# A one-core SwiGLU kernel: the first x block and the first gate weights loaded in halves of D

## The chip, the cores and the metric

The kernel runs on one NeuronCore of a Trainium2 chip. The metric is the device time of one execution in microseconds (us), lower is better. Where several executions were timed, the median is given.

## The reference

```
x [1, 2048, 512], w_gate [512, 1376], w_up [512, 1376], w_down [1376, 512], all bf16
g = silu(x @ w_gate)
u = x @ w_up
return (g * u) @ w_down
```

D is 512 (the contraction of the first two products), F is 1376 (the contraction of the last one), and S is 2048 tokens.

## The kernel before

**Tiling.** The tokens are cut into 4 chunks `c` of 512. F is cut into 10 whole tiles `ft` of 128 and a rest of 96. A "G" group computes gate for one tile and one chunk: four matmuls, one for each slice `dk` of 128 of D, with 128x128 weights from `w_sb` and 512 tokens of the transposed x (`xT_sb`) as the moving operand. A "U" group does the same for up. ScalarE (ACT) applies silu to the G bank, VectorE (DVE) multiplies it with the U bank and writes `hT_sb`. The rests of F go through groups "X" and "Y". After all chunks, "O" groups compute the down product from `hT_sb` and `wd_sb`, DVE copies them to `o_sb`, and SP stores them.

**Who orders what.** The program is written out by hand for each engine, with semaphores between the engines: `s_P` counts PE's groups, `s_A` ACT's, `s_D` DVE's operations, and every load has a semaphore of its own. PE runs its instructions in the written order. The helper `need(name)` makes PE wait for a load, and `after(eng, n)` for the n-th operation of ACT or DVE.

**The start**, which is where the change lies:

- SP's queue issues, in this order: `xn` (the first 256 tokens of x as they lie in memory, 128 partitions of 2 KB, L108), the gate and the up weights of tile 1 (L92), `x0b` (tokens 256 to 511 through a transposing load, L87), then gate and up weights of tiles 2 and 3, 4 to 6, 7 to the rest, then the other chunks of x and w_down. ACT's queue issues the gate and the up weights of tile 0 (L92). Each of the first four weight loads is a slab of one tile: 512 pieces of 256 bytes, 128 KB.
- PE first runs matmuls on constants whose result nobody reads (L337): `N_WARM` = 6 of 512 columns and `N_FILL` = 2 of 128 columns. Then it waits for `xn` and transposes it, 8 transposes of 128x128 (L346) in 4 groups "T". A group is one block `i` of 128 tokens and one half `h` of D, in the order (i0,h0), (i0,h1), (i1,h0), (i1,h1).
- The 4 groups are copied from PSUM to `xT_sb`: h0 by DVE (L293), h1 by ACT (L280).
- Then PE runs the first halves (tokens 0 to 255) of the groups g0, u0 (in blocks of 128 columns, all four `dk` of a block in turn), g1, u1 (256 columns), and after `x0b` the second halves of all four (L328, 256 columns). From tile 2 on every matmul has 512 columns.

Of the kernel before, what the change touches and what calls it, by code (L numbers as in the profile page):

```python
# [6 lines left out]
BF16 = mybir.dt.bfloat16  # L7
FP32 = mybir.dt.float32

N_WARM = 6  # L10
N_FILL = 2


def bass_standalone__swiglu_ffn__prompt_kernel(nc, x, w_gate, w_up, w_down, out):
    _, S, D = x.shape
    F = w_gate.shape[1]
    P = 128
    KD = D // P
    NFF = F // P
    NFT = NFF + 1  # L20
    F_LAST = F - NFF * P
    SC = 512
# [4 lines left out]
    NR = 3  # L27
    LASTA = 384
    HT = SC // 2
    NXN = HT // P  # L30
    NB = 8
    NSG = 4
# [3 lines left out]
    xf = x[0]  # L36
# [3 lines left out]
    UPH = F + 32  # L40
# [4 lines left out]
    with ExitStack() as es:  # L45
# [4 lines left out]
        xT_sb = sb("xT_sb", [P, KD, S], BF16)  # L50
        w_sb = sb("w_sb", [P, KD, WTOT], BF16)
# [12 lines left out]

        xn_sb = sb("xn_sb", [P, NXN, D], BF16)
        ident = sb("ident", [P, P], BF16)
# [10 lines left out]
        def load_sem(name):  # L77
            loads[name] = sem(f"s_{name}")
            return loads[name]
# [6 lines left out]
        def load_x(eng, name, t0, t1):  # L86
            eng.dma_start_transpose(  # L87
                xT_sb[:, :, t0:t1], xf[t0:t1, :]
            ).then_inc(load_sem(name), 16)

        def load_w(eng, name, src, base, f0, f1):
            eng.dma_start(  # L92
                w_sb[:, :, base + f0:base + f1],
                src[:, f0:f1].rearrange("(k p) f -> p k f", p=P),
            ).then_inc(load_sem(name), 16)

        slabs = [(0, 1), (1, 2), (2, 4), (4, 7), (7, NFT)]
        slab_of = {ft: a for a, b in slabs for ft in range(a, b)}

        def load_slab(eng, a, b):  # L100
            load_w(eng, f"wg{a}", w_gate, 0, a * P, min(b * P, F))
            load_w(eng, f"wu{a}", w_up, UPH, a * P, min(b * P, F - 32))

        def loads_on_scalar(act):
            load_slab(act, *slabs[0])

        def loads_on_sync(sp):
            sp.dma_start(  # L108
                xn_sb[:, :, :].rearrange("p j d -> p (j d)"), xf[0:HT, :].rearrange("(p j) d -> p (j d)", j=NXN)
            ).then_inc(load_sem("xn"), 16)  # L110
            load_slab(sp, *slabs[1])
            load_x(sp, "x0b", HT, SC)
            for a, b in slabs[2:]:
                load_slab(sp, a, b)
            load_w(sp, "wut", w_up, F - (F - 32), F - 32, F)
            for c in range(1, NSC):
                load_x(sp, f"x{c}", c * SC, (c + 1) * SC)
            sp.dma_start(
                wd_sb[:, 0:NFF, :], w_down[0:NFF * P, :].rearrange("(k p) d -> p k d", p=P)
            ).then_inc(load_sem("wd"), 16)  # L120
            for c in range(NSC):
                sp.dma_start(
                    wdt_sb[R * c:R * (c + 1), :, :], w_down[NFF * P:F, :].rearrange("(q p) d -> p q d", p=R)
                ).then_inc(load_sem(f"wdt{c}"), 16)
            sp.dma_start(wdl_sb[:, :], w_down[NFF * P:F, LASTA:D]).then_inc(load_sem("wdl"), 16)
# [7 lines left out]
        def add_group(kind, **what):  # L133
            g = dict(kind=kind, at=len(groups), bank=banks[len(groups) % NB], readers=[], **what)
            groups.append(g)
            return g

        def add_op(eng, g, **what):
            n_read[eng] += 1
            op = dict(g=g, at=n_read[eng], **what)  # L140
            (act_ops if eng == "A" else dve_ops).append(op)
            g["readers"].append((eng, op["at"]))
            return op

        def tview(bank):
            return bank[:, 0:P].bitcast(BF16).rearrange("p (k t) -> p k t", k=2)
# [58 lines left out]
                t_ready[c] = d["at"]  # L205

        xt_ready = {}
        for i in range(NXN):
            for h, eng in enumerate("DA"):
                g = add_group("T", i=i, h=h)  # L210
                op = add_op(
                    eng, g, kind="copy", out=xT_sb[:, 2 * h:2 * h + 2, i * P:(i + 1) * P],
                    src=tview(g["bank"]), stored=(None, 0),
                )
                xt_ready[i, h] = (eng, op["at"])
# [12 lines left out]
        for at in range(NST):  # L228
            j, c = divmod(at, NSC)
            t = c * TPC + j  # L230
            ob = at % NOS
            need = 16 * n_store[ob]
            halves = [(0, D)] if at < NST - 1 else [(0, LASTA), (LASTA, D)]
            for c0, c1 in halves:
                g = add_group("O", t=t, c0=c0, c1=c1, c=c)
                if c0 == 0:
                    quads[j].append(g)
                else:
                    last = g
                eng = "A" if len(halves) == 2 and c0 == 0 else "D"  # L240
                op = add_op(
                    eng, g, kind="copy", out=o_sb[ob][:, c0:c1], src=g["bank"][:, 0:c1 - c0],
# [6 lines left out]
        def rows_of(t):  # L249
            if t < NXN:  # L250
                return of[0:HT, :].rearrange("(p j) d -> j p d", j=NXN)[t]
            return of[t * P:(t + 1) * P, :]

        def on_sync(sp):
            loads_on_sync(sp)
            for t, c0, c1, ob, eng, n in stores:
                sp.wait_ge(s_A if eng == "A" else s_D, n)
                sp.dma_start(rows_of(t)[:, c0:c1], o_sb[ob][:, c0:c1]).then_inc(s_out[ob], 16)
            for i in range(NOS):
                sp.wait_ge(s_out[i], 16 * n_store[i])  # L260
# [6 lines left out]
        def on_scalar(act):  # L267
            loads_on_scalar(act)
            act.activation(adummy[:, 0:4], zero_c, ACT.Silu)  # L269
            for op in act_ops:  # L270
                act.wait_ge(s_P, op["g"]["at"] + 1)
                if op["kind"] == "silu":
                    if op["free"]:
                        act.wait_ge(s_D, op["free"])
                    fn = ACT.Silu
                else:
                    if op["stored"][1]:
                        act.wait_ge(*op["stored"])
                    fn = ACT.Copy
                act.activation(op["out"], op["src"], fn).then_inc(s_A, 1)  # L280
# [15 lines left out]
        def on_tensor(pe):  # L296
            landed = set()

            def need(name):
                if name not in landed:  # L300
                    pe.wait_ge(loads[name], 16)
                    landed.add(name)
# [3 lines left out]
            def after(eng, n):  # L306
                if n > read[eng]:
                    pe.wait_ge(s_A if eng == "A" else s_D, n)
                    read[eng] = n
# [3 lines left out]
                    for eng, n in groups[g["at"] - NB]["readers"]:  # L313
                        after(eng, n)

            def gu_matmuls(g, n0, n1):
                c, ft = g["c"], g["ft"]
                if c > 0:
                    need(f"x{c}")
                if c == 0 and n1 > HT:  # L320
                    need("x0b")
                need(("wg" if g["kind"] == "G" else "wu") + str(slab_of[ft]))
                col = (0 if g["kind"] == "G" else UPH) + ft * P
                for dk in range(KD):
                    if c == 0 and dk % 2 == 0:
                        for i in range(n0 // P, min(n1 // P, NXN)):
                            after(*xt_ready[i, dk // 2])
                    ins = pe.matmul(  # L328
                        g["bank"][:, n0:n1], lhsT=w_sb[:, dk, col:col + P],
                        rhs=xT_sb[:, dk, c * SC + n0:c * SC + n1], start=(dk == 0), stop=(dk == KD - 1),  # L330
                    )
                if n1 == SC:
                    ins.then_inc(s_P, 1)

            def warm(n, width):
                for i in range(n):
                    pe.matmul(banks[NB - 1][:, 0:width], lhsT=ones_w, rhs=ones_m[:, 0:width], start=True, stop=True)  # L337

            warm(N_WARM, SC)
            warm(N_FILL, P)  # L340
            pe.wait_ge(s_J, 1)
            need("xn")
            for g in groups[:NT]:
                for k in range(2):
                    dk = 2 * g["h"] + k
                    ins = pe.transpose(tview(g["bank"])[:, k, :], xn_sb[:, g["i"], dk * P:(dk + 1) * P], ident[:, :])  # L346
                ins.then_inc(s_P, 1)

            g0, u0, g1, u1 = groups[NT:NT + 4]
            for g in (g0, u0):  # L350
                gu_matmuls(g, 0, P)
                gu_matmuls(g, P, HT)
            gu_matmuls(g1, 0, HT)
            gu_matmuls(u1, 0, HT)
            for g in (g0, u0, g1, u1):
                gu_matmuls(g, HT, SC)

            for g in groups[NT + 4:]:
                kind = g["kind"]
# [5 lines left out]
                elif kind == "X":  # L365
                    c = g["c"]
                    need(f"wg{slab_of[NFF]}")
                    need("wut")
                    for dk in range(KD):
                        ins = pe.matmul(  # L370
                            g["bank"][:, :], lhsT=w_sb[:, dk, XC0:XC0 + P],
                            rhs=xT_sb[:, dk, c * SC:(c + 1) * SC],
                            start=(dk == 0), stop=(dk == KD - 1),
                        )
                    ins.then_inc(s_P, 1)
                elif kind == "Y":
                    need(f"wu{slab_of[NFF]}")
                    for dk in range(KD):
                        for c in (2 * g["pi"], 2 * g["pi"] + 1):
# [3 lines left out]
                                rhs=xT_sb[:, dk, c * SC:(c + 1) * SC],  # L383
                                start=(dk == 0), stop=(dk == KD - 1),
# [33 lines left out]
            for j in range(0, TPC, 2):  # L418
# [14 lines left out]
                skip_group_check=True,  # L433
# [35 lines left out]
```

## Time and profile before

| | |
|---|---|
| three timed runs | 120.83, 120.94, 120.31 us; median 120.83 us |
| the profiled execution | 120.32 us |
| span of its trace, first to last instruction | 118.9 us (1.42 us of its time lie around the span) |
| PE busy (matmul) | 115.4 us, 97% of the span |
| DVE, ACT busy | 47.3 us (40%), 31.0 us (26%) |
| loads and stores | 8.84 MB, mean 74 GB/s; the DMA engines are busy through the first 27 us of the span and nearly idle from there to 89 us |

Engines in the profile: PE is the matmul row of TensorE, PEld its weight loads, SPq and ACTq the instructions that SP and ACT issue to DMA queues. L328 is line 328 of the kernel. A row of a timeline gives the start, the duration, what ran, how many were merged, and in brackets the idle time before and what ended it. The duration of one matmul is from its start to the end of its result, so back-to-back matmuls overlap; their pace is the distance from start to start.

### The profile page before, as it was taken

What the parts mean: (1) busy time and instruction counts of PE and PEld (TensorE: products, weight loads), DVE (VectorE), ACT (ScalarE), POOL (GpSimd) and SP (SyncE); (2) the same over time, 40 slices, a digit from 0 to 9 for tenths busy, and PEclk for the clock granted to TensorE, in tenths of its full rate; (3) what the DMA queues carried; (4) which work ended last, traced back from release to release, by engine and by line L of the source; (5) the groups of instructions that cost most, each with busy time, mean ns of one, the idle gap of its engine ahead of it and who ended that gap; (6) DMA issues with size and microseconds to landing.
All of it is one profiled execution on the core that took longest, in us unless ns stands there. A gap on an engine that the chain in (4) does not pass through costs nothing.

```text
span 118.9 us, 1519 instructions
## 1 busy us (share of the span) xinstructions
PE 115.4 (97%) x600; PEld 54.1 (45%) x611; DVE 47.3 (40%) x73; ACT 31.0 (26%) x53; POOL 0.4 (0%) x5
## 2 busy tenths in 40 slices
PE   7999999999999999999999999999999999999993
PEld 2774444444444444444444444344434444444452
DVE  0133443353443444433444334469617422006530
ACT  4344324454234363244262343230000000000001
POOL 1000000000000000000000000000000000000000
PEclk9999999999999999999999999999999999999999
DMA  3999999970000000000000000000004221002412
GB/s 103 271 307 357 264 162 242 328 183 24 0 0 0 6 0 0 0 3 3 0 0 0 6 0 0 0 0 0 0 0 138 88 88 44 0 0 75 145 50 88
DMA packets 17559, 8.84 MB, mean 74 GB/s; under 512 B 10640, under 2 KB 17424, under 8 KB 17552
## 3 DMA queue, kind: packets, MB, share of 16 engines
q1 hardware_dynamic: 16496, 8.48, 26.7%
q10 hardware_dynamic: 1056, 0.26, 1.0%
q8 instruction: 5, 0.08, 0.3%
q14 instruction: 2, 0.02, 0.1%
HBM read 4.81 MB, written 2.10 MB: 58 GB/s over the span
## 4 chain that ended last, share of the span: by engine, by line
PE 97%; issue 1%; DVE 0%
PE bank L328 58%; PE bank L394 29%; PE bank L370 3%; PE bank L337 2%; PE bank L408 2%; PE bank L381 2%; PE bank L346 1%; DVE o_sb L293 0%; PE bank L431 0%
## 5 line engine op out<-in xcount | busy, mean ns | idle before, releaser
L328 PE MATMUL bank<-xT_sb,w_sb 128*128 128x512 bf16 (+2 forms) x338 | 69.7, 364 | 0.4
L328 PEld LDWEIGHTS bank<-xT_sb,w_sb 128*128 128x128 bf16 x344 | 32.8, 98 | 36.4 <-issue 0.2
L289 DVE TENSOR_TENSOR hT_sb<-sg_sb,bank 128x512 bf16<-128x512 f32 x40 | 27.5, 688 | 40.5 <-PE bank L328 36.6
L394 PE MATMUL bank<-wd_sb,hT_sb 128*128 128x512 bf16 (+2 forms) x166 | 34.5, 366 | 0.4 <-issue 0.3
L280 ACT ACTIVATE sg_sb<-bank 128x512 f32<-128x512 f32 x40 | 23.8, 596 | 40.8 <-PE bank L328 40.8
L394 PEld LDWEIGHTS bank<-wd_sb,hT_sb 128*128 128x128 bf16 x170 | 16.1, 98 | 19.1 <-issue 1.3
L293 DVE CAST o_sb<-bank 128x512 bf16<-128x512 f32 (+1 forms) x16 | 10.1, 663 | 22.0 <-PE bank L408 12.3
L280 ACT ACTIVATE o_sb<-bank 128x384 bf16<-128x384 f32 x1 | 0.5, 492 | 37.8 <-PE bank L394 37.8
L289 DVE TENSOR_TENSOR ht_sb<-sgy_sb,bank 32x512 bf16<-32x512 f32 x8 | 5.5, 684 | 0.2
L289 DVE TENSOR_TENSOR ht_sb<-sgx_sb,bank 32x512 bf16<-32x512 f32 x4 | 2.8, 691 | 3.5 <-ACT sgx_sb L280 3.5
L370 PE MATMUL bank<-xT_sb,w_sb 128*128 128x512 bf16 x15 | 4.1, 379 | 0.1
L337 PE MATMUL bank<-const-bfloat16-1.0 128*128 128x512 bf16 (+1 forms) x8 | 2.9, 545 | 0.8 <-PEq L454 0.8
L280 ACT ACTIVATE sgx_sb<-bank 32x512 f32<-32x512 f32 x4 | 2.4, 588 | 4.5 <-PE bank L370 4.5
L408 PE MATMUL bank<-wdt_sb,ht_sb 32*128 32x512 bf16 (+1 forms) x48 | 2.9, 372 | 0.0
L370 PEld LDWEIGHTS bank<-xT_sb,w_sb 128*128 128x128 bf16 x16 | 1.6, 98 | 1.9
L280 ACT ACTIVATE sgy_sb<-bank 64x512 f32<-64x512 f32 x4 | 2.4, 590 | 0.1
L337 PEld LDWEIGHTS bank<-const-bfloat16-1.0 128*128 128x128 bf16 x8 | 1.0, 136 | 2.4 <-issue 2.4
L381 PE MATMUL bank<-xT_sb,w_sb 128*64 128x512 bf16 x16 | 1.9, 382 | 0.0
L408 PEld LDWEIGHTS bank<-wdt_sb,ht_sb 32*128 32x128 bf16 x48 | 1.1, 93 | 1.7 <-issue 0.8
L269 ACT ACT_TABLE_LOAD x1 | 1.3, 1283 | 1.8 <-issue 1.8
L293 DVE COPY xT_sb<-bank 128x256 bf16<-128x256 bf16 x2 | 0.6, 292 | 2.7 <-PE bank L346 2.7
L381 PEld LDWEIGHTS bank<-xT_sb,w_sb 128*64 128x64 bf16 x16 | 0.8, 109 | 1.0 <-DVE hT_sb L289 0.4
(14 smaller groups left out, 4.0 us busy)
## 6 DMA issues: line engine op xcount, KB each, us to landing
out_dram<-o_sb SPq DMA_DIRECT2D x15, 128.0 KB, 1.7
wd_sb<-in_w_down_dram SPq DMA_DIRECT2D x1, 1280.0 KB, 9.2
w_sb<-in_w_gate_dram SPq DMA_DIRECT2D x1, 480.0 KB, 5.9
w_sb<-in_w_up_dram SPq DMA_DIRECT2D x1, 448.0 KB, 6.5
w_sb<-in_w_gate_dram SPq DMA_DIRECT2D x1, 384.0 KB, 4.5
w_sb<-in_w_up_dram SPq DMA_DIRECT2D x1, 384.0 KB, 5.1
wdt_sb<-in_w_down_dram SPq DMA_DIRECT2D x4, 96.0 KB, 7.5
xn_sb<-in_x_dram SPq DMA_DIRECT2D x1, 256.0 KB, 2.8
```

Source lines behind the costliest of these rows:

```text
L269: act.activation(adummy[:, 0:4], zero_c, ACT.Silu)
L280: act.activation(op["out"], op["src"], fn).then_inc(s_A, 1)
L289: ins = dve.tensor_tensor(op["out"], op["a"], op["b"], ALU.mult)
L293: ins = dve.tensor_copy(op["out"], op["src"])
L328: ins = pe.matmul(g["bank"][:, n0:n1], lhsT=w_sb[:, dk, col:col + P], rhs=xT_sb[:, dk, c * SC + n0:c * SC + n1], start=(dk == 0), stop=(dk ...
L337: pe.matmul(banks[NB - 1][:, 0:width], lhsT=ones_w, rhs=ones_m[:, 0:width], start=True, stop=True)
L346: ins = pe.transpose(tview(g["bank"])[:, k, :], xn_sb[:, g["i"], dk * P:(dk + 1) * P], ident[:, :])
L370: ins = pe.matmul(g["bank"][:, :], lhsT=w_sb[:, dk, XC0:XC0 + P], rhs=xT_sb[:, dk, c * SC:(c + 1) * SC], start=(dk == 0), stop=(dk == KD - 1),
L381: ins = pe.matmul(g["bank"][y0:y1, :], lhsT=w_sb[:, dk, YC0:YC0 + 64], rhs=xT_sb[:, dk, c * SC:(c + 1) * SC], start=(dk == 0), stop=(dk == ...
L394: ins = pe.matmul(g["bank"][:, 0:c1 - c0], lhsT=hT_sb[:, fk, t * P:(t + 1) * P], rhs=wd_sb[:, fk, c0:c1], start=(start and fk == 0), stop= ...
L408: ins = pe.matmul(g["bank"][:, 0:c1 - c0], lhsT=ht_sb[R * c:R * (c + 1), q, j * P:(j + 1) * P], rhs=wdt_sb[R * c:R * (c + 1), q, c0:c1], s ...
```

## The change

The first 256 tokens of x come in two loads of 256 values of D each (`xn0`, `xn1`; 256 pieces of 512 bytes each) on SP's queue. The slabs of tiles 0 and 1 become one slab of two tiles. Its gate weights come in two loads of half of D each (`wg0h0`, `wg0h1`; 256 pieces of 512 bytes) on ACT's queue, its up weights in one load (`wu0`; 512 pieces of 512 bytes) on SP's queue. The constant matmuls become 5 and 1. The T groups are ordered h0 first: (h0,i0), (h0,i1), (h1,i0), (h1,i1), the first of each pair copied by DVE, the second by ACT, and PE waits for `xn1` only between the two pairs. Then g0 and g1 run in blocks of 128 columns: steps `dk` 0 and 1 of all blocks first, then steps 2 and 3 of all blocks; then u0 and u1 in 256 columns. The matmuls are the same in number and shape (16 of 128 columns, 24 of 256 columns); only their order and which groups use which shape differ. `start` marks the first matmul written to a bank only.

```diff
-N_WARM = 6
-N_FILL = 2
+N_WARM = 5
+N_FILL = 1
+NEARLY = 2
...
-        slabs = [(0, 1), (1, 2), (2, 4), (4, 7), (7, NFT)]
+        slabs = [(0, 2), (2, 4), (4, 7), (7, NFT)]
...
+        def load_w_half(eng, name, src, base, f0, f1, h):
+            eng.dma_start(
+                w_sb[:, 2 * h:2 * h + 2, base + f0:base + f1],
+                src[2 * h * P:2 * (h + 1) * P, f0:f1].rearrange("(k p) f -> p k f", p=P),
+            ).then_inc(load_sem(name), 16)
...
         def loads_on_scalar(act):
-            load_slab(act, *slabs[0])
+            for h in range(2):
+                load_w_half(act, f"wg0h{h}", w_gate, 0, 0, slabs[0][1] * P, h)

         def loads_on_sync(sp):
-            sp.dma_start(
-                xn_sb[:, :, :].rearrange("p j d -> p (j d)"), xf[0:HT, :].rearrange("(p j) d -> p (j d)", j=NXN)
-            ).then_inc(load_sem("xn"), 16)
-            load_slab(sp, *slabs[1])
+            for h in range(2):
+                sp.dma_start(
+                    xn_sb[:, :, h * HD:(h + 1) * HD],
+                    xf[0:HT, h * HD:(h + 1) * HD].rearrange("(p j) d -> p j d", j=NXN),
+                ).then_inc(load_sem(f"xn{h}"), 16)
+            load_w(sp, "wu0", w_up, UPH, 0, slabs[0][1] * P)
             load_x(sp, "x0b", HT, SC)
-            for a, b in slabs[2:]:
+            for a, b in slabs[1:]:
                 load_slab(sp, a, b)
...
-        for i in range(NXN):
-            for h, eng in enumerate("DA"):
+        for h in range(2):
+            for i, eng in enumerate("DA"):
                 g = add_group("T", i=i, h=h)
...
-            def gu_matmuls(g, n0, n1):
+            def gu_matmuls(g, n0, n1, dks=range(KD), start=True):
...
-                for dk in range(KD):
+                for dk in dks:
+                    if g["kind"] == "G" and slab_of[ft] == 0:
+                        need(f"wg0h{dk // 2}")
...
-                        rhs=xT_sb[:, dk, c * SC + n0:c * SC + n1], start=(dk == 0), stop=(dk == KD - 1),
+                        rhs=xT_sb[:, dk, c * SC + n0:c * SC + n1], start=(start and dk == 0), stop=(dk == KD - 1),
...
             pe.wait_ge(s_J, 1)
-            need("xn")
             for g in groups[:NT]:
+                need(f"xn{g['h']}")
...
-            for g in (g0, u0):
-                gu_matmuls(g, 0, P)
-                gu_matmuls(g, P, HT)
-            gu_matmuls(g1, 0, HT)
-            gu_matmuls(u1, 0, HT)
+            for h in range(2):
+                for i in range(NXN):
+                    for g in (g0, g1):
+                        gu_matmuls(g, i * P, (i + 1) * P, range(2 * h, 2 * h + 2), start=(i == 0))
+            for g in (u0, u1):
+                gu_matmuls(g, 0, HT)
             for g in (g0, u0, g1, u1):
-                gu_matmuls(g, HT, SC)
+                gu_matmuls(g, HT, SC, start=False)
```

More of the change, by code (lines that the diff above doesn't have):

```diff
@@ L29, in bass_standalone__swiglu_ffn__prompt_kernel @@
     HT = SC // 2
+    HD = D // 2
     NXN = HT // P
@@ L321, in gu_matmuls @@
                     need("x0b")
-                need(("wg" if g["kind"] == "G" else "wu") + str(slab_of[ft]))
+                if g["kind"] == "U" or slab_of[ft] > 0:
+                    need(("wg" if g["kind"] == "G" else "wu") + str(slab_of[ft]))
                 col = (0 if g["kind"] == "G" else UPH) + ft * P
-                for dk in range(KD):
+                for dk in dks:
+                    if g["kind"] == "G" and slab_of[ft] == 0:
+                        need(f"wg0h{dk // 2}")
                     if c == 0 and dk % 2 == 0:
@@ L329, in gu_matmuls @@
                         g["bank"][:, n0:n1], lhsT=w_sb[:, dk, col:col + P],
-                        rhs=xT_sb[:, dk, c * SC + n0:c * SC + n1], start=(dk == 0), stop=(dk == KD - 1),
+                        rhs=xT_sb[:, dk, c * SC + n0:c * SC + n1], start=(start and dk == 0), stop=(dk == KD - 1),
+                        skip_group_check=(ft < NEARLY and c == 0),
                     )
```

## The prediction

> **What bounds the kernel now.** I read the page's busy times and its chain first.
>
> ```profile
> PE 115.4 (97%) x600; PEld 54.1 (45%) x611; DVE 47.3 (40%) x73; ACT 31.0 (26%) x53; POOL 0.4 (0%) x5
> PE 97%; issue 1%; DVE 0%
> PE bank L328 58%; PE bank L394 29%; PE bank L370 3%; PE bank L337 2%; PE bank L408 2%; PE bank L381 2%; PE bank L346 1%; DVE o_sb L293 0%; PE bank L431 0%
> ```
>
> TensorE is the chain from start to end. A faster load can therefore gain only before PE's stream has become dense, and one row of the chain gives nothing useful: L337, 2.93 us of matmuls on constants. So the question is when useful work starts, and what it waits for. The timeline of the first 8 us (rows of other engines left out):
>
> ```profile
> 0.74 0.40 SPq L108 DMA_DIRECT2D xn_sb<-in_x_dram  x1
> 0.77 2.93 PE L337 MATMUL bank<-const-bfloat16-1.0 128*128 128x512 bf16 x8 [0.77 <-PEq L454]
> ...
> 2.44 0.15 PEld L337 LDWEIGHTS bank<-const-bfloat16-1.0 128*128 128x128 bf16 x1 [0.28 <-issue]
> 2.86 0.15 PEld L337 LDWEIGHTS bank<-const-bfloat16-1.0 128*128 128x128 bf16 x1 [0.28 <-issue]
> ...
> 3.63 0.78 PE L346 MATMUL bank<-ident,xn_sb 128*128 128x128 bf16 x8
> ...
> 4.04 0.59 DVE L293 COPY xT_sb<-bank 128x256 bf16<-128x256 bf16 x2 [2.72 <-PE bank L346]
> 4.22 0.66 ACT L280 ACTIVATE xT_sb<-bank 128x256 bf16<-128x256 bf16 x2 [0.94 <-PE bank L346]
> 4.44 1.81 PEld L328 LDWEIGHTS bank<-xT_sb,w_sb 128*128 128x128 bf16 x24 [0.21 <-issue]
> 4.47 3.87 PE L328 MATMUL bank<-xT_sb,w_sb 128*128 128x128 bf16 x40
> ...
> 6.42 1.86 PEld L328 LDWEIGHTS bank<-xT_sb,w_sb 128*128 128x128 bf16 x18 [0.17 <-DMA xT_sb<-in_x_dram]
> ```
>
> Useful work starts at 3.63 with the transposes. The first gate matmul starts at 4.47, because the last transpose started at about 4.19 and the copies had to follow. At 6.42 PE has waited a moment for `x0b`. The time to landing, added to the issue's start, says which load ends each wait (DMA view of the issues from 0.5 to 2.3 us; the last column is us to landing):
>
> ```profile
> xn_sb<-in_x_dram SPq DMA_DIRECT2D x1, 256.0 KB, 2.8
> w_sb<-in_w_gate_dram ACTq DMA_DIRECT2D x1, 128.0 KB, 3.2
> w_sb<-in_w_up_dram SPq DMA_DIRECT2D x1, 128.0 KB, 3.7
> xT_sb<-in_x_dram SPq DMA_TRANSPOSE x1, 4.2
> ```
>
> So `xn` lands at 0.74 + 2.8 = 3.54, just ahead of the transposes; gate 0 at 0.73 + 3.2 = 3.93; up 1 at 1.66 + 3.7 = 5.36; `x0b` at 2.20 + 4.2 = 6.40, just ahead of 6.42. Everything later is early: gate and up of tiles 2, 3 land at 3.94 + 3.3 = 7.24 and 4.56 + 3.5 = 8.06 and are used from about 8.2 and 9.05. After 6.42 the chain has no gap worth naming.
>
> Two paces matter. Constant matmuls of 512 columns start 2.86 - 2.44 = 0.42 to 0.43 us apart, while in mid-kernel 48 matmuls take 10.36 us, 0.216 each. So PE starts at half pace: 0.107 against 0.055 us per 128 columns. The eight transposes take 0.78 with a last duration of 0.22, that is 0.56 for seven steps: three or four at 0.107, the rest at 0.055. PE came to full pace at about 4.0.
>
> **The loads, part by part.** Bytes and their order hardly differ: five loads and then `x0b`, SP's fourth issue before and after. Before, xn, gate 0, gate 1, up 0, up 1 are 786 KB ahead of `x0b`; after, xn0, wg0h0, xn1, wg0h1, wu0 are again 786 KB. ACT issues two loads ahead of its table load in both; POOL issues none. What differs is the piece: 2 KB (xn) and 256 B (weights) become 512 B throughout. Three windows of the DMA view have one size each (2 KB, 256 B, 512 B):
>
> ```profile
> DMA packets 73, 0.15 MB, mean 299 GB/s; under 512 B 0, under 2 KB 0, under 8 KB 73
> ```
> ```profile
> DMA packets 2191, 0.55 MB, mean 273 GB/s; under 512 B 2191, under 2 KB 2191, under 8 KB 2191
> ```
> ```profile
> DMA packets 652, 0.33 MB, mean 326 GB/s; under 512 B 16, under 2 KB 652, under 8 KB 652
> ```
>
> Before, 0.262 MB at 299 and 0.524 MB at 273 GB/s take 0.88 + 1.92 = 2.80 us; after, 0.786 MB at 326 take 2.41. So `wu0` lands 0.39 earlier than up 1 did, at about 4.97, and `x0b`, whose own load is as before (0.262 MB in 256 B pieces, 0.96 us), at about 6.01.
>
> The single landings: the moving starts about 1.8 us (the trace's transfer rate is zero before it), and up 1 landed 5.36 - 1.8 - 2.80 = 0.76 after its share of the bytes. `xn` gives the other bound: alone it needed 0.88 and landed 0.86 later; if gate 0 shared all the way (1.36 us) it landed 0.38 later. With a tail of 0.4 to 0.86: xn0 (0.131 MB, 0.40 us) lands at 2.6 to 3.1. xn1, with wg0h0 between (0.393 MB, 1.21), lands at 3.4 to 3.9; I take 3.65, the middle, as no row has two queues with 512 B pieces in the first microsecond. wg0h0 lands at 3.0 to 3.5, wg0h1 at 3.8 to 4.3.
>
> **TensorE, part by part.** Constants: one of 512 and one of 128 columns fewer, 0.427 + 0.107 = 0.53 us, so they end near 2.97 instead of 3.50. This is worth nothing by itself; it opens the place for xn0.
>
> h0 transposes: four at half pace, 0.43 us, from about 3.1 to 3.55. Before, four took this at 3.63. Their copies (DVE 0.29, ACT 0.38, the rows' halves) run beside the wait for xn1. ACT's table load and dummy end near 3.3, so they hide as well.
>
> h1 transposes: they wait for xn1, the one new wait. All gate matmuls stand behind it on PE although the first half of them needs only h0, and both h1 copies behind that. From 3.65 + 0.1 = 3.75: two or three at half pace, the rest at full, to about 4.1.
>
> Gates: steps 0, 1 of g0 and g1, 8 x 0.055 = 0.45 us, run 4.13 to 4.6. They cover the h1 copies: DVE's from about 4.2 to 4.5, ACT's from 4.3 to 4.7, needed at 4.6 and 4.82. The exposed time between transposes and gates of before (0.78 - 0.22 + 3.63 + 0.06 = 4.25 to 4.47, 0.22 us, and about 0.15 more inside the first gates, whose 16 matmuls of 128 columns took 4.46 to 5.50, 1.04 us against 16 x 0.055 = 0.88) goes. Gates end at 5.05. Ups: 8 of 256 columns x 0.109 = 0.87, to 5.92; wu0 at 4.97 is just in time. `x0b` at about 6.01 is then late by 0.1: that is the next wait, and it takes a fifth of the gain. Second halves start at about 6.02 instead of 6.42: 0.40 gained. If the wait is nil, 0.50.
>
> From there on nothing holds PE back: tiles 2, 3 land 0.39 earlier too (6.85 against a use at 7.8), tokens 512 to 1023 land at 8.86 + 8.1 = 17 and are used at 23.0. All of it reaches the end. I take 0.42: profiled 120.32 - 0.42 = 119.90. The profiled execution is 0.51 under the median; from the median, 120.83 - 0.42 = 120.4.
>
> [...] In the trace, the change to full pace came at about 4.0, 3.2 us after the first constant matmul. [...]
>
> **Rivals.**
>
> *All waits hidden* (18%). xn0 and xn1 land one after the other, gate loads behind them. xn1 then lands at 1.8 + 0.80 + 0.4 = 3.0; transposes run 3.1 to 3.95, gates from 4.0 to 4.9, ups to 5.75, and x0b at its early bound (1.8 + 2.41 + 0.96 + 0.4 = 5.57) is no wait. Gain 0.67: 120.16. For it: xn's 2 KB pieces moved 0.15 MB in a window in which only its queue appears. Against it: gate 0 landed only 0.39 after xn.
>
> *Full pace comes late* (21%, slower). If PE's rise needs an unbroken run as long as the one seen (3.2 us) and the gap before xn1 starts it anew at 3.75, full pace comes at 7.0. From 4.0 to 7.0 work runs at half pace: 1.5 us lost, 0.42 gained, so +1.1: 121.9. It decides as soon as the gap counts at all; a median over runs of both kinds lies between.
>
> *The halves do not do what they say* (11%). xn1 lands late, and as the h1 transposes stand ahead of every gate matmul, the early half buys only four transposes. Each 0.1 us of xn1 past 3.9 costs 0.1; at 4.4 the gain is gone: 120.8.
>
> The first case has 50%.
>
> **How the numbers follow.** About 0.5% (0.6 us) is what a measurement here can tell from no change; the three runs of before lie 0.63 apart. The forecast's 0.42 is under this bound, and with that scatter passes it in about two of five: 0.19 faster, 0.31 same. Waits hidden: 0.16 faster, 0.02 same. Late pace: 0.21 slower. Late half: 0.09 same, 0.02 slower. Sums: faster 0.35, same 0.42, slower 0.23. The range reaches from the hidden case less most of the scatter (120.16 - 0.5, 119.6) to just under the late-pace price, 121.8; the likeliest case alone is 120.0 to 120.8.
>
> **What would show it.** Right: a constants row ending near 3.2, four transposes near 3.1 and four near 3.75, gate matmuls without a gap from 4.15, L328's first wait at `x0b` near 6.0, span about 118.5. Wrong: matmul rows of 256 columns longer than 0.273 us after 4.1 (late pace), h1 transposes after 3.9 (late half), an idle PEld before the ups (wu0 late), or `x0b` not earlier than 6.4, which alone would bring the gain to nothing.

## The result and the profile after

The changed kernel takes 122.40 us (median of 15 runs, 121.11 to 123.25) against 120.54 us (15 runs, 120.31 to 121.04). The ratio is 1.0136, 95% interval 1.0113 to 1.0159: slower by 1.4%, where a gain of 0.42 us (0.35%), less than can be told from no change, was forecast. Ratios and intervals, here and below, leave out executions more than 1.5% above the shortest of the same kernel (here 122.98 and 123.25 us), so 1.0136 is not quite the quotient of the two medians, 1.015. The profiled execution is the longest of the 15 (123.25 us, span 121.8), so what is added up in it comes to more than the median shows; what it shows of the pace is seen again below in executions of 122.12 to 123.11 us that the ratios include.

The page, busy times and chain:

```profile
PE 116.9 (96%) x598; PEld 55.4 (45%) x609; DVE 47.3 (39%) x73; ACT 31.1 (26%) x53; POOL 0.4 (0%) x5
PE 94%; DMA 3%; issue 1%; SPq 1%; DVE 0%
PE bank L342 58%; PE bank L410 28%; DMA xn_sb<-in_x_dram 3%; PE bank L386 3%; PE bank L424 2%; PE bank L397 2%; SPq L118 1%; PE bank L361 1%; DVE o_sb L304 0%; PE bank L447 0%
```

The chain now goes through a load, `xn_sb` with 3% of the span, and the issue of it (L118). The constants have left the chain: TensorE no longer works from the start to the end without a break. PE is also busy 1.5 us longer (116.9 against 115.4), with two constant matmuls fewer. The timeline of the start shows where:

```profile
0.73 0.97 ACTq L103 DMA_DIRECT2D w_sb<-in_w_gate_dram  x2
0.74 1.30 SPq L118 DMA_DIRECT2D xn_sb<-in_x_dram  x2
0.77 2.40 PE L352 MATMUL bank<-const-bfloat16-1.0 128*128 128x512 bf16 x6 [0.77 <-PEq L470]
...
2.09 0.60 SPq L94 DMA_DIRECT2D w_sb<-in_w_up_dram  x1
...
3.78 0.58 PE L361 MATMUL bank<-ident,xn_sb 128*128 128x128 bf16 x4 [0.60 <-DMA xn_sb<-in_x_dram]
...
5.16 0.61 PE L361 MATMUL bank<-ident,xn_sb 128*128 128x128 bf16 x4 [0.80 <-DMA xn_sb<-in_x_dram]
...
5.56 5.68 PE L342 MATMUL bank<-xT_sb,w_sb 128*128 128x128 bf16 x40
```

Two waits for halves of x stand in the brackets, before the transposes at 3.78 and at 5.16. The landings, from a DMA view of the issues at 0.5 to 0.8 us and one at 1.3 to 2.8 us (last column: us from issue to landing):

```profile
xn_sb<-in_x_dram SPq DMA_DIRECT2D x1, 128.0 KB, 2.9
```
```profile
xn_sb<-in_x_dram SPq DMA_DIRECT2D x1, 128.0 KB, 3.7
w_sb<-in_w_up_dram SPq DMA_DIRECT2D x1, 256.0 KB, 4.2
xT_sb<-in_x_dram SPq DMA_TRANSPOSE x1, 4.6
```

`xn0` lands at 0.74 + 2.9 = 3.64, no earlier than the whole of x did before (3.54). `xn1`, whose issue starts only at 1.45, lands at 5.1. The up load lands at 2.09 + 4.2 = 6.3 and `x0b` at 2.74 + 4.6 = 7.3.

The second thing is the pace. Groups of PE by form, from 5.1 to 9.6 us (columns: busy us, mean ns of one | idle us before):

```profile
L342 PE MATMUL bank<-xT_sb,w_sb 128*128 128x256 bf16 x11 | 2.6, 421 | 0.0
L342 PE MATMUL bank<-xT_sb,w_sb 128*128 128x128 bf16 x16 | 1.9, 314 | 0.0
```

The same forms in the kernel before (4.02 to 14 us):

```profile
L328 PE MATMUL bank<-xT_sb,w_sb 128*128 128x256 bf16 x24 | 2.8, 273 | 0.0
L328 PE MATMUL bank<-xT_sb,w_sb 128*128 128x128 bf16 x16 | 1.2, 220 | 0.1
```

In the changed kernel PE runs at half pace through all of this stretch. Over the first 11.2 us the 24 matmuls of 256 columns average 343 ns, so about 11 ran at 421 and 13 at 273; from 7.27 on at 0.213 us each, full pace comes at about 9.7 us, against 4.0 before.

In this execution the loss is complete when the tiles go over to 512 columns: the first such matmul starts at 11.29 us against 8.40, 2.9 us later, as in the spans (121.8 less 118.9). From 5.16 to there, half pace costs 0.18 (4 transposes) + 0.83 (16 of 128 columns) + 0.84 (8 of 256) + about 0.36 (the rest up to 9.7), some 2.2 us; the other 0.7 us are the late start.

### The profile page after: what moved, and what is told of

Read it like the earlier page. It is cut to its first block, busy times and chain, and to the rows that moved or that the text cites. A ratio compares the mean times of both kernels' runs of the same rounds, so it can differ in the third digit from the quotient of the medians.

```text
span 121.8 us, 1516 instructions
## 1 busy us (share of the span) xinstructions
PE 116.9 (96%) x598; PEld 55.4 (45%) x609; DVE 47.3 (39%) x73; ACT 31.1 (26%) x53; POOL 0.4 (0%) x5
## 4 chain that ended last, share of the span: by engine, by line
PE 94%; DMA 3%; issue 1%; SPq 1%; DVE 0%
PE bank L342 58%; PE bank L410 28%; DMA xn_sb<-in_x_dram 3%; PE bank L386 3%; PE bank L424 2%; PE bank L397 2%; SPq L118 1%; PE bank L361 1%; DVE o_sb L304 0%; PE bank L447 0%
## 5 line engine op out<-in xcount | busy, mean ns | idle before, releaser
L342 PE MATMUL bank<-xT_sb,w_sb 128*128 128x512 bf16 (+2 forms) x338 | 71.5, 373 | 0.3
L342 PEld LDWEIGHTS bank<-xT_sb,w_sb 128*128 128x128 bf16 x344 | 34.4, 102 | 36.5
L304 DVE CAST o_sb<-bank 128x512 bf16<-128x512 f32 (+1 forms) x16 | 10.1, 664 | 22.0 <-PE bank L424 12.3
L352 PE MATMUL bank<-const-bfloat16-1.0 128*128 128x512 bf16 (+1 forms) x6 | 2.4, 573 | 0.8 <-PEq L470 0.8
L361 PE MATMUL bank<-ident,xn_sb 128*128 128x128 bf16 x8 | 1.2, 304 | 1.4 <-DMA xn_sb<-in_x_dram 1.4
L386 PEld LDWEIGHTS bank<-xT_sb,w_sb 128*128 128x128 bf16 x16 | 1.6, 98 | 1.9
L361 PEld LDWEIGHTS bank<-ident,xn_sb 128*128 128x128 bf16 x8 | 0.7, 129 | 2.2 <-issue 1.2
```

The costliest lines, as they stand in the source:

```text
L304: ins = dve.tensor_copy(op["out"], op["src"])
L342: ins = pe.matmul(g["bank"][:, n0:n1], lhsT=w_sb[:, dk, col:col + P], rhs=xT_sb[:, dk, c * SC + n0:c * SC + n1], start=(start and dk == 0) ...
L386: ins = pe.matmul(g["bank"][:, :], lhsT=w_sb[:, dk, XC0:XC0 + P], rhs=xT_sb[:, dk, c * SC:(c + 1) * SC], start=(dk == 0), stop=(dk == KD - 1),
```

## The experiments

Two theories. *Clock*: full pace comes late, because PE has less work and a gap in its first microseconds. *Loads*: x and the weights land later, and useful work starts later. The clock theory has two forms: a gap of half a microsecond already counts, or one so short mostly passes and only a longer one counts. All experiments copy tokens 256 and up plainly instead of transposing them, so the products of those tokens are of other numbers; the diffs after the first two leave this edit out. Each kernel has one profiled execution. A control of each kernel shows that this leaves the difference as it is.

**The kernel before, plain copy.**

```diff
-            eng.dma_start_transpose(
-                xT_sb[:, :, t0:t1], xf[t0:t1, :]
+            eng.dma_start(
+                xT_sb[:, :, t0:t1],
+                xf[t0:t1, :].rearrange("(p a) d -> p (a d)", p=P).rearrange("p (k c) -> p k c", k=KD),
             ).then_inc(load_sem(name), 16)
```

> Control: the kernel before, but tokens 256 and up of x are copied into xT_sb as they lie in memory (512-byte and 1 KB pieces), not transposed; the products of those tokens are therefore of other numbers, the work is the same. All experiments share this. If those loads don't matter for the time: 120.4 to 120.7 us, 0.998 to 1.002 of before.

Measured: 120.43 us, 0.9992 (0.9970 to 1.0014). Same as before.

**The changed kernel, plain copy** (the same edit).

> Control: the changed kernel with the same plain copy of tokens 256 and up. Both theories, clock (full pace of PE comes late, as its start has less work and gaps) and loads (x and weights land later): the loss stays, 121.6 to 122.6 us, 1.010 to 1.017 of before. If the transposing load that follows at once behind the halves is the cause: 120.5 us or less.

Measured: 123.09 us, 1.0161 (1.0085 to 1.0238). The loss stays, in the median above the range expected. That the transposing load was its cause is out. In the profile (123.11 us) `xn0` landed at 3.9 and `xn1` at 4.6, and PE was idle only once, ahead of the first transposes:

```profile
4.00 1.23 PE L362 MATMUL bank<-ident,xn_sb 128*128 128x128 bf16 x8 [0.83 <-DMA xn_sb<-in_x_dram]
```
```profile
L343 PE MATMUL bank<-xT_sb,w_sb 128*128 128x256 bf16 x24 | 4.4, 366 | 0.0
```

The gates start earlier than in the profile of the changed kernel (5.02 against 5.56), yet the 256-column matmuls average 366 ns (first 11.2 us): full pace comes only at about 10.1 us.

**The changed kernel with PE kept busy.**

```diff
-N_WARM = 5
-N_FILL = 1
+N_WARM = 7
+N_FILL = 0
+N_MID = 3
...
             for g in groups[:NT]:
+                if g["h"] == 1 and g["i"] == 0:
+                    warm(N_MID, SC)
                 need(f"xn{g['h']}")
```

> The changed kernel (plain copy of tokens 256 and up) with PE kept busy: 7 constant matmuls of 512 columns ahead (to about 3.75 us) and 3 more between the h0 and the h1 transposes, where PE waits for xn1; loads and order as changed. Clock theory: full pace at about 4 to 5 us in place of 9.7, the clock's share of the loss goes, only the later loads stay, 120.9 to 121.6 us, 1.003 to 1.009. Loads theory: nothing comes back, 122.2 to 122.6 us, 1.013 to 1.017.

Measured: 121.38 us, 1.0059 (1.0037 to 1.0082). Over half of the loss goes with work that computes nothing, so it cannot have been loads alone. In the profile the h1 transposes start at 5.48, and the 16 gate matmuls behind them take 0.95 us: full pace from about 5.8 (groups by form, 5.4 to 7 us).

```profile
L344 PE MATMUL bank<-xT_sb,w_sb 128*128 128x128 bf16 x16 | 1.1, 218 | 0.0
```

**The changed kernel with x in one load, constants 6 and 2.**

```diff
-N_WARM = 5
-N_FILL = 1
+N_WARM = 6
+N_FILL = 2
...
-            for h in range(2):
-                sp.dma_start(
-                    xn_sb[:, :, h * HD:(h + 1) * HD],
-                    xf[0:HT, h * HD:(h + 1) * HD].rearrange("(p j) d -> p j d", j=NXN),
-                ).then_inc(load_sem(f"xn{h}"), 16)
+            sp.dma_start(
+                xn_sb[:, :, :].rearrange("p j d -> p (j d)"), xf[0:HT, :].rearrange("(p j) d -> p (j d)", j=NXN)
+            ).then_inc(load_sem("xn"), 16)
...
-                need(f"xn{g['h']}")
+                need("xn")
```

> The changed kernel (plain copy of tokens 256 and up) with the first 256 tokens of x in one load again (2 KB pieces) and the constants 6 and 2; gate halves, merged up and the new PE order stay. If the halves of x are the cause, through either theory: xn lands at 3.5, PE has no gap, full pace at 4.0, and the gates and the up load come in time: 120.1 to 120.5 us (0.996 to 1.000). If the weights in new pieces or the new order are the cause: 121.5 us and more (1.008 or more).

Measured: 120.55 us, 1.0004 (0.9979 to 1.0029). Gate halves, merged up load and the new order cost nothing when x comes whole. They gain nothing either: the up load landed at 1.18 + 4.0 = 5.2 and `x0b` at 1.65 + 5.0 = 6.6, later than the 6.40 of before.

**The kernel before with fewer constants**, two runs:

```diff
-N_WARM = 6
-N_FILL = 2
+N_WARM = 5
+N_FILL = 1
```
```diff
-N_WARM = 6
-N_FILL = 2
+N_WARM = 3
+N_FILL = 0
```

> The kernel before (plain copy of tokens 256 and up) with only the constants cut to 5 and 1, so PE is idle from about 3.0 to 3.6 us; every other load and the order as before. Clock theory in the form that a gap of half a microsecond already counts: 121.3 to 122.1 us (1.007 to 1.013). [...] Loads theory: no change (1.000).

> The kernel before (plain copy of tokens 256 and up) with only 3 constants of 512 columns, so PE is idle from about 2.05 to 3.6 us; the loads and the useful work as before, useful work starts at the same moment. Clock theory, either form: full pace moves from about 4 to 6 or later, 121.3 to 122.3 us (1.007 to 1.015) with no load any later. Loads theory: no change, 120.5 us (1.000).

Measured: with 5 and 1, 120.61 us, 1.0012 (0.9984 to 1.0040); with 3, 121.65 us, 1.0094 (1.0053 to 1.0136). The second shows the clock theory by itself, with no load moved. PE's timeline of that run, and its groups by form from 6.1 to 8.7 us:

```profile
0.77 1.44 PE L338 MATMUL bank<-const-bfloat16-1.0 128*128 128x512 bf16 x3 [0.77 <-PEq L455]
3.63 1.01 PE L347 MATMUL bank<-ident,xn_sb 128*128 128x128 bf16 x8 [1.42 <-DMA xn_sb<-in_x_dram]
4.48 6.82 PE L329 MATMUL bank<-xT_sb,w_sb 128*128 128x128 bf16 x45
```
```profile
L329 PE MATMUL bank<-xT_sb,w_sb 128*128 128x256 bf16 x12 | 2.8, 420 | 0.0
```

Transposes start at 3.63 and gates at 4.48, to 0.01 us as in the kernel before; only the constants are fewer. Yet the matmuls of 256 columns still take 420 ns. The single times fall in two groups, five at 121.03 to 121.19 and five at 122.12 to 122.65. With 5 and 1, seven of ten lie at 120.83 or less and three at 121.27 to 121.32. The profiled execution with 5 and 1 (121.32 us) is one of the three: PE was idle for 0.68 us and came to full pace at about 6.7. So in this kernel a gap of 0.6 to 0.7 us mostly passed; with one of 1.42 us all ten executions are 0.4 us or more above the median of before (120.58).

**The queues exchanged** (x halves on ACT, gate halves on SP).

```diff
         def loads_on_scalar(act):
             for h in range(2):
-                load_w_half(act, f"wg0h{h}", w_gate, 0, 0, slabs[0][1] * P, h)
+                act.dma_start(
+                    xn_sb[:, :, h * HD:(h + 1) * HD],
+                    xf[0:HT, h * HD:(h + 1) * HD].rearrange("(p j) d -> p j d", j=NXN),
+                ).then_inc(load_sem(f"xn{h}"), 16)
         def loads_on_sync(sp):
             for h in range(2):
-                sp.dma_start(
-                    xn_sb[:, :, h * HD:(h + 1) * HD],
-                    xf[0:HT, h * HD:(h + 1) * HD].rearrange("(p j) d -> p j d", j=NXN),
-                ).then_inc(load_sem(f"xn{h}"), 16)
+                load_w_half(sp, f"wg0h{h}", w_gate, 0, 0, slabs[0][1] * P, h)
```

> The changed kernel (plain copy of tokens 256 and up) with the queues of its halves exchanged: ACT issues the two halves of x, SP the two gate halves, the up load and the rest. If the x halves are late because SP's queue is served behind ACT's: xn0 lands near 3.2, xn1 near 4.0, the gates near 3.6 and 4.5; the wait before the h1 transposes shrinks, 121.3 to 122.0 us (1.006 to 1.012). If they are late because half rows of x in 512-byte pieces are slow to fetch, on any queue: xn0 at 3.6 or later again, no gain over the changed kernel (1.013 or more).

Measured: 122.97 us, 1.0212 (1.0162 to 1.0262). Timeline rows of the issues:

```profile
0.73 1.28 ACTq L115 DMA_DIRECT2D xn_sb<-in_x_dram  x2
0.74 0.95 SPq L104 DMA_DIRECT2D w_sb<-in_w_gate_dram  x2
```

The long issue (0.62 and 0.64 us) and the late landing (xn0 at 3.5, xn1 at 5.6) move to ACT with the x halves, and the gate halves on SP are quick. The queue is not the cause.

**x split by tokens** (pieces of 1 KB, one per partition and load).

```diff
-            for h in range(2):
-                sp.dma_start(
-                    xn_sb[:, :, h * HD:(h + 1) * HD],
-                    xf[0:HT, h * HD:(h + 1) * HD].rearrange("(p j) d -> p j d", j=NXN),
-                ).then_inc(load_sem(f"xn{h}"), 16)
+            for j in range(NXN):
+                sp.dma_start(
+                    xn_sb[:, j, :], xf[0:HT, :].rearrange("(p j) d -> j p d", j=NXN)[j]
+                ).then_inc(load_sem(f"xn{j}"), 16)
...
-        for h in range(2):
-            for i, eng in enumerate("DA"):
+        for i in range(NXN):
+            for h, eng in enumerate("DA"):
...
-                need(f"xn{g['h']}")
+                need(f"xn{g['i']}")
```

> The changed kernel (plain copy of tokens 256 and up) with the two loads of x split by tokens in place of by D (128 pieces of 1 KB each, one per partition), the transposes in the order of the token blocks; constants 5 and 1, gate halves, merged up and the order of the gates as changed. If two loads as such cost the time (the second is a DMA of its own, behind the gate half): 122 us and more (1.012 or more). If the two-piece pattern of the D halves costs it (issue of 0.6 us, first bytes 0.5 us later): xn0 lands near 2.9, xn1 near 3.6, little gap, 120.4 to 121.0 us (0.999 to 1.004).

Measured: 120.92 us, 1.0027 (1.0002 to 1.0052). With the same short constants and two loads of the same size, most of the loss is gone: the loads land 2.6 us after issue in the mean (3.2 and 3.9), and the gaps before the transposes are short. Full pace came at about 4.1 in the profile. What that execution (121.68 us, the longest of the ten) lost, it lost to the merged up load, which landed 5.2 us after its issue, at 6.9:

```profile
6.92 4.30 PE L342 MATMUL bank<-xT_sb,w_sb 128*128 128x256 bf16 x31 [1.40 <-DMA w_sb<-in_w_up_dram]
```

**The halves of D alone**, in the kernel before.

```diff
-            sp.dma_start(
-                xn_sb[:, :, :].rearrange("p j d -> p (j d)"), xf[0:HT, :].rearrange("(p j) d -> p (j d)", j=NXN)
-            ).then_inc(load_sem("xn"), 16)
+            for h in range(2):
+                sp.dma_start(
+                    xn_sb[:, :, h * (D // 2):(h + 1) * (D // 2)],
+                    xf[0:HT, h * (D // 2):(h + 1) * (D // 2)].rearrange("(p j) d -> p j d", j=NXN),
+                ).then_inc(load_sem(f"xn{h}"), 16)
...
-            need("xn")
             for g in groups[:NT]:
+                need(f"xn{g['h']}")
```

> The kernel before (plain copy of tokens 256 and up) with one part of the change alone: the first 256 tokens of x in two loads by halves of D; constants 6 and 2, weights and order as before, so the first transposes wait for xn0 and the third for xn1. If the halves of D are the root of the loss, through late landings and then the gap: xn1 lands at 4.4 to 5.1, the gap of PE before it is 0.8 us or more, 121.3 to 122.5 us (1.006 to 1.015). If the loss needs the short constants or the new weights as well: 120.5 to 121.0 us (1.000 to 1.004).

Measured: 122.20 us, 1.0146 (1.0103 to 1.0189). This one part costs as much as the whole change. Here constants 6 and 2 were kept; in the profile xn1 landed at 5.1, and from the third transpose on, at 5.18, PE was at full pace:

```profile
5.18 0.51 PE L349 MATMUL bank<-ident,xn_sb 128*128 128x128 bf16 x6 [0.91 <-DMA xn_sb<-in_x_dram]
```

The last wait is for `x0b`, issued at 3.25 instead of 2.21, as two issues of x of 0.63 and 0.59 us stand ahead of it in place of one of 0.40, and landed at 8.0. The first matmul of 512 columns starts at 10.00, 1.5 us later than in the control (8.47). So lateness alone cost 1.5 us in this execution (121.93 us); how the pace stood in the longer ones (122.47 and 122.88) is not known.

**Rows of a partition 128 apart.**

```diff
-                    xf[0:HT, h * HD:(h + 1) * HD].rearrange("(p j) d -> p j d", j=NXN),
+                    xf[0:HT, h * HD:(h + 1) * HD].rearrange("(j p) d -> p j d", j=NXN),
```

> The changed kernel (plain copy of tokens 256 and up) with the rows of each partition's two blocks 128 rows apart in memory in place of neighbours (the blocks of tokens are permuted, pieces and sizes stay: 256 of 512 bytes per half). If the long issue (0.64 us) and the late first bytes belong to two half rows that lie close together: issue 0.45 us as for the gate halves, first bytes near 1.8, xn0 at 3.1, xn1 near 4.0, 121 to 121.8 us (1.004 to 1.010). If they belong to any pattern of two pieces of x per partition: as the changed kernel, 122 us or more (1.012 or more).

Measured: 122.41 us, 1.0148 (1.0113 to 1.0183). The issue came as in the first case, the landings 0.3 and 0.5 us later than it had them, the time as in the second. Timeline rows:

```profile
0.74 0.94 SPq L119 DMA_DIRECT2D xn_sb<-in_x_dram  x2
...
3.56 0.58 PE L362 MATMUL bank<-ident,xn_sb 128*128 128x128 bf16 x4 [0.39 <-DMA xn_sb<-in_x_dram]
...
4.55 0.61 PE L362 MATMUL bank<-ident,xn_sb 128*128 128x128 bf16 x4 [0.41 <-DMA xn_sb<-in_x_dram]
```

Two issues take 0.94 us instead of 1.30, xn0 lands at 0.74 + 2.7 = 3.4, xn1 at 1.23 + 3.3 = 4.5, and both waits are shorter than in the profile of the changed kernel. SP's queue moves its first packet at 1.82 us, against 2.33 there. But PE is still idle twice, and the matmuls of 256 columns average 358 ns in this run: full pace at about 9.7. Half pace costs 0.18 (4 transposes) + 0.83 (16 of 128 columns) + about 1.6 (14 of 256) = 2.6 us, all of what the first matmul of 512 columns starts later than before (10.96 against 8.40). With the loads of x mended, the pace alone keeps the loss.

**The changed kernel with constants 6 and 2.**

```diff
-N_WARM = 5
-N_FILL = 1
+N_WARM = 6
+N_FILL = 2
```

> The changed kernel (plain copy of tokens 256 and up) with only the constants put back to 6 and 2. [...] Loads theory: as the changed kernel (1.014 to 1.018).

Measured: 121.53 us, 1.0083 (1.0055 to 1.0112). Part of the loss goes with the constants alone. PE's timeline:

```profile
5.36 0.40 PE L362 MATMUL bank<-ident,xn_sb 128*128 128x128 bf16 x4 [0.92 <-DMA xn_sb<-in_x_dram]
...
7.18 4.09 PE L343 MATMUL bank<-xT_sb,w_sb 128*128 128x256 bf16 x29 [0.45 <-DMA w_sb<-in_w_up_dram]
```

The four h1 transposes take 0.40 us, so PE is at full pace from 5.36 on, although it had been idle for 0.92 us just before. What is left in this execution (121.96 us) are two late loads: `xn1` at 5.3 and the merged up load at 7.1.

**Both mended: rows 128 apart and PE kept busy** (against the changed kernel).

```diff
-N_WARM = 5
-N_FILL = 1
+N_WARM = 6
+N_FILL = 2
+N_MID = 1
...
-                    xf[0:HT, h * HD:(h + 1) * HD].rearrange("(p j) d -> p j d", j=NXN),
+                    xf[0:HT, h * HD:(h + 1) * HD].rearrange("(j p) d -> p j d", j=NXN),
...
+                if g["h"] == 1 and g["i"] == 0:
+                    warm(N_MID, SC)
```

> The changed kernel (plain copy of tokens 256 and up) with both suspected causes taken away at once: rows of a partition's two blocks 128 rows apart (tokens permuted), which brought the halves of x to 3.42 and 4.51, and PE kept busy by constants 6 and 2 ahead and one of 512 columns between the pairs of transposes. If the late full pace is what the same loads still cost without the constants (1.0148): 120.4 to 121.0 us (0.999 to 1.004). If the halves and the order cost something beside the pace and the landings seen: 121.3 us and more (1.007 or more).

Measured: 121.10 us, 1.0059 (1.0039 to 1.0079), between the two cases. At nearly equal landings of x (3.5 and 4.3 here), keeping PE busy is worth 1.0148 - 1.0059 = 0.9%, 1.1 us. The rest shows in PE's timeline of this run:

```profile
4.72 1.13 PE L344 MATMUL bank<-xT_sb,w_sb 128*128 128x128 bf16 x16
6.44 3.87 PE L344 MATMUL bank<-xT_sb,w_sb 128*128 128x256 bf16 x28 [0.59 <-DMA w_sb<-in_w_up_dram]
```

The gates run at full pace (16 in 1.13 us) and end near 5.7, but the merged up load, issued at 1.74, lands 4.7 us later, at 6.4, and PE waits. At half pace, in the run with the rows apart alone, the gates lasted until 6.7 and the up load, landed at 6.1, was not waited for.

**In addition the up load in two.**

```diff
-            load_w(sp, "wu0", w_up, UPH, 0, slabs[0][1] * P)
+            for ft in range(2):
+                load_w(sp, f"wu{ft}t", w_up, UPH, ft * P, (ft + 1) * P)
...
-                if g["kind"] == "U" or slab_of[ft] > 0:
+                if g["kind"] == "U" and slab_of[ft] == 0:
+                    need(f"wu{ft}t")
+                elif slab_of[ft] > 0:
```

> The run with both causes taken away (rows 128 apart, PE kept busy), and in addition up of tiles 0 and 1 in two loads of 256-byte pieces as before the change, each waited for by its own tile. If the merged up load (landed 6.40, PE waited 0.8 us for it) is the rest of the loss: up 0 near 5.3, up 1 near 5.9, 120.3 to 120.8 us (0.999 to 1.002). If the time at which bytes arrive is the same whatever the load is cut into: up 1 at 6.4 again, then tokens 256 up, 120.9 to 121.2 us (1.004 to 1.006).

Measured: 120.88 us, 1.0015 (0.9988 to 1.0041). Up landed at 5.3 and 5.8, as in the first case, and PE did not wait for it. The loss is gone within what can be told, though the median lies between the two cases, and this interval and the one before it touch at 1.004. All parts mended, the new order is still no gain. The profiled execution (121.19 us, the third longest of ten) also shows what the constants do not secure. Groups by form, 4.8 to 6.4 us:

```profile
L347 PE MATMUL bank<-xT_sb,w_sb 128*128 128x128 bf16 x16 | 1.7, 294 | 0.0
```

Constants and waits are as in the run before, PE is idle nowhere between its first constant and these gates, and yet full pace came at about 6.2 instead of 4.6.

**Try at a better version**: the kernel before with x split by tokens and constants 5 and 4.

```diff
-N_WARM = 6
-N_FILL = 2
+N_WARM = 5
+N_FILL = 4
...
-            sp.dma_start(
-                xn_sb[:, :, :].rearrange("p j d -> p (j d)"), xf[0:HT, :].rearrange("(p j) d -> p (j d)", j=NXN)
-            ).then_inc(load_sem("xn"), 16)
+            for j in range(NXN):
+                sp.dma_start(
+                    xn_sb[:, j, :], xf[0:HT, :].rearrange("(p j) d -> j p d", j=NXN)[j]
+                ).then_inc(load_sem(f"xn{j}"), 16)
...
-            need("xn")
             for g in groups[:NT]:
+                need(f"xn{g['i']}")
```

> Try at a better version: the kernel before (plain copy of tokens 256 and up) with the first 256 tokens of x in two loads by token blocks (1 KB pieces), and constants 5 and 4, ending near 3.3 us; weights and order as before. xn0 landed at 3.16 and xn1 at 3.92 in the token split seen so far: four transposes start 0.3 us earlier, the other four 0.3 us later than before, the gates are bound by gate 0 at 3.9 to 4.1 as before. Expected 120.3 to 120.7 us (0.998 to 1.002): no loss, and hardly a gain.

Measured: 120.57 us, 1.0005 (0.9986 to 1.0024). No loss and no gain. No version that I ran beats the kernel before.

## Why the prediction was wrong

- **Chain and place**: right. The whole difference arises before tile 2, and nothing later takes part.
- **Landings of the halves**: the first step that failed. xn0 was put at 2.6 to 3.1 and landed at 3.64; xn1 at 3.4 to 3.9, taken as 3.65, and landed at 5.1. The term was bytes over a rate plus a tail, with the issue of one x load (0.40 us) carried over to its halves. An issue of a half took 0.66 us, the next one started at 1.45 instead of 1.20, SP's queue moved its first packet at 2.33 where the sum has bytes moving from 1.8, and the first half was no quicker than the whole. The runs show that this belongs to the halves of D of neighbouring rows: with the same pieces from rows 128 apart, issue 0.43 us and landings at 3.4 and 4.5; with the queues exchanged it moves along with x. The issue is the firm part, 0.59 to 0.66 us against 0.43 to 0.45 in every profile. The landing of xn1 scatters: 4.6 in the control of the changed kernel, 5.1 to 5.6 in the five other profiles with neighbouring rows, 4.3 to 4.5 in the three with the rows apart.
- **786 KB at 326 GB/s**: failed as well. `wu0` was put at 4.97 and `x0b` at 6.01; they landed at 6.3 and 7.3. The rate of a steady stretch was used for a stretch in which the DMA engines were partly idle (changed kernel, windows; columns: length, PE busy, granted clock, DMA share, GB/s):

```profile
2.97:3.78 0.81, 0.21 (x3) 1.00 1.04 295
3.78:4.46 0.68, 0.58 (x4) 1.00 0.59 127
```

From 3.78 to 4.46 the DMA engines moved 127 GB/s and were idle for 0.4 of the time, with 512 pieces of up long issued. In the changed kernel nobody waited for `wu0`, as PE was at half pace; of the four profiles with the merged up load, x in two loads and gates at full pace, three have a wait of PE for it (1.40, 0.45 and 0.59 us). The clock column stands at 1.00 in a stretch in which PE ran at half pace, so the pace is read from the matmul rows.
- **Full pace at about 4.0 in the sum**: failed, and in the profiled execution this is the larger part, 2.2 of 2.9 us. It was carried over from before, and came at 9.7. It stood as the slower rival, with 21% and +1.1 us from an unbroken run of 3.2 us counted anew at 3.75. Sign and mechanism, idle PE putting off the rise, were right: keeping PE busy is worth 0.9% at nearly equal landings, and fewer constants alone cost 0.9% (1.0094). What was off is the gap that counts. The rival starts its run anew at the gap before xn1 and has full pace 3.2 us behind it; in the profiles the rise goes with the gap ahead of the first transposes. Where PE was idle for at most 0.2 us there (ten profiles), full pace came by 6.2 us, in two of them in spite of 0.9 us idle before xn1; where it was idle for 0.39 to 1.42 us (six profiles), it came at 6.7 to 10.1, in the control of the changed kernel, with no second gap, 6.1 us after the transposes began at 4.00. So an unbroken run of 3.2 us is not what decides; that it is the first gap is read from one execution of each kernel, not tested by a run of its own. The weight was off too, and the range ended at 121.8, just under this rival's price. The sum's own gaps were 0.13 and 0.2 us (2.97 to 3.1, 3.55 to 3.75); any lateness of xn0 or xn1 widens them, so late landings and late pace were one case, not two independent ones.
- **The moment of full pace**: early idle time put it off in these runs (with 3 constants, matmuls of 256 columns still took 420 ns from 6.1 to 8.7, against 273 in the control of the kernel before), but it also varied between starts that look alike: with at most 0.2 us idle ahead of the first transposes it lay anywhere from before 3.7 us (x in one load, where the weight loads of the eight transposes, from 3.71 on, took 0.46 us against 0.63 in the kernel before) to 6.2 us (up in two), that is from less than 2.9 to 5.4 us after the first constant matmul. How much idle time put it off the runs only bound: in the kernel before, 0.6 to 0.7 us idle mostly passed, 1.42 us did not.
- **Gates' stalls of before (0.22 and 0.15 us)**: the saving did appear. The 16 gate matmuls and the transposes of the changed kernel follow each other without a gap (5.16 to 7.27), but at half pace, where the copies have nearly twice the time (the 16 gate matmuls run 1.71 us, 5.56 to 7.27, against 0.95 in the run with PE kept busy), and it was outweighed.
- **"All waits hidden" and "halves do not do what they say"**: the first did not occur. The second did, beyond its price: xn1 passed the 4.4 at which the gain was to be gone.
- **The signs**: three of the four signs named for "wrong" came: 256-column rows of 421 ns after 4.1, h1 transposes after 3.9 (at 5.16), and `x0b` later than 6.4 (at 7.3), though nobody waited for it, because PE was later still.

What stays open: why half rows of neighbouring rows take longer to issue and to land, why the merged up load lands so late behind x in two loads (6.1 to 7.1 in eight profiles) when it landed at 5.2 behind x in one, and what sets the moment of full pace between executions with the same start. The shares of lateness and pace are not additive: at half pace PE hid a wait that showed at full pace (for the merged up load none with the rows apart alone, 0.59 us with PE kept busy as well), so 0.9% for the pace holds for the mended landings only.

## What to carry to other kernels

Before cutting a first load in pieces so as to start earlier, ask what the engine does between the pieces: here the constants ahead of the load did a job, as they brought TensorE to full pace earlier (matmuls of 256 columns from 6.1 to 8.7 took 420 ns with 3 constants; behind 6 and 2 all 24 took 273), and leaving it idle twice for 0.4 us in place of constants cost about 1.1 us at nearly equal landings. Price a piece of a transfer by the landing of a piece of that form (for `xn0` here: issue 0.66 us, first packet of its queue at 2.33, landing at 3.64, where 2.6 to 3.1 was forecast), not by bytes over the rate of a busy stretch. Read the pace of TensorE from the same matmul form at two places (256 columns here: 421 and 273 ns).

## What was not expected of the hardware

- A load of 256 pieces of 512 bytes took 0.59 to 0.66 us to issue when the two pieces of a partition were half rows of neighbouring rows of 1 KB, and 0.43 to 0.45 us when the rows lay 128 apart. The first half landed 2.8 to 3.1 us after the start of its issue in the one case and 2.7 in the other, the second 3.1 to 4.3 and 3.0 to 3.3.
- Two kernels with the same useful work from the same moment differed by 0.9% only because one had 1.5 us less of constant matmuls ahead of it.
- With nearly the same unbroken work from the start, TensorE came to full pace at about 4.6 us in one profiled execution and at 6.2 us in another.
- Runs of one kernel with gaps at the start scatter by 2 us (the changed kernel, 121.11 to 123.25) or fall in two groups 1 us apart (the kernel before with 3 constants); the kernel before, without gaps, stays within 0.73 us in its 15 runs.
